# Attention and squared-ReLU FFN on one core: three score bursts instead of four in one group, and the second batch's values loaded behind w_in

## The chip, the cores and the metric

The kernel runs on one core of a Trainium2 chip. The metric is the device time of one execution in microseconds (us), as the median of several runs. The engines are named as in the profile: PE is TensorE (matmuls), PEld its weight loads, ACT is ScalarE, DVE is VectorE, POOL is GpSimd, SP is SyncE. "L367" is a line of the kernel. Lines after 570 differ by three between the two kernels; those quoted most (L341 score matmuls, L351 exponentials, L367 attention times values, "AV", L425 and L462 the first FFN matmul, L524 the second) are the same in both.

## The reference

Grouped-query attention, heads put side by side, then an FFN with a squared ReLU. Outputs and inputs are float32. (Shortened here.)

```python
def _attn_ref(q, k, v):               # q (8,16,384,64), k and v (8,4,384,64)
    k = np.repeat(k, 4, axis=1); v = np.repeat(v, 4, axis=1)
    scores = np.matmul(q, k.transpose(0, 1, 3, 2)) / np.sqrt(64)
    attn = np.exp(scores - scores.max(-1, keepdims=True))
    attn = attn / (attn.sum(-1, keepdims=True) + 1e-09)
    return np.matmul(attn, v)

def reference(q, k, v, moe_w_in, moe_w_out):      # w_in (1024,2048), w_out (2048,1024)
    a = _attn_ref(q, k, v)
    x = a.transpose(0, 2, 1, 3).reshape(8 * 384, 1024)
    h = np.maximum(x @ moe_w_in, 0.0)
    return h * h @ moe_w_out
```

## The kernel before

The program is built by a small scheduler. It appends instructions to the five engines with its own estimates of when each is ready, always takes the most urgent candidate that is ready, and picks a PSUM bank for each tile. What comes out is a fixed instruction list for each engine. So a change in one place of the source can move the order of everything after it.

A score "burst" is the set of score matmuls that one exponential reads. The first batch's attention runs at the start, with pieces of its first FFN matmul (four "early" output tiles) as filler. Then the second batch's scores are mixed with the rest of that matmul, twelve tiles in three groups of four ("quads"). Then come the second batch's AV and the first batch's second FFN matmul, and so on.

```python
    def burst_small(b, pieces, base):          # scores of some key units, then one exponential
        def sc(pe):
            for m, (u, _, _) in enumerate(pieces):
                for x in range(2):
                    mm = pe.matmul(ps[:, base + x, m * wide:(m + 1) * wide],
                                   kT[b % 2][64 * x:64 * x + 64, u, :], q_cols(b, u // NJ, x, c0, c0 + wide))
            return mm
        # ... tensor op, then on ScalarE:
        R.add("scalar", lambda e: e.activation(dst, src, AF.Exp, scale=0.125), reads=keys, ...)

    def pick(allowed):                          # which PSUM bank
        turn_count[0] += 1
        i = min(allowed, key=lambda i: (max(R.when(writes=[("bank", i)]), R.clock["tensor"]), used[i]))
        used[i] = turn_count[0]
        return i

    # ... the order of GpSimd's loads at the start
    load_q(1, 0, 8)
    load_q(1, 8, 16)
    load_w_in(1)
    load_v(1)
    dup_k(1)
    for i in range(2, 6):
        load_w_in(i)
    aug_v(1, "gpsimd")                          # waits for load_v(1)
    for i in range(6, 8):
        load_w_in(i)
    load_w_out(0, 0)
    load_w_out(0, 1)

    # ... the first batch's bursts: (key unit, first column, columns)
    for group in ((0, 1), (2, 3), (4, 5), (6, 7), (8, 9), (10, 11)):
        if 0 < group[0] < NU - 2:
            smalls += [[(u, 0, 512)] for u in group] + [[(u, 512, 256) for u in group]]
        else:
            smalls += [[(u, c0, 384)] for c0 in (0, 384) for u in group]

    # ... when an AV is taken
            b, c = av_q.pop(0)
            av_open = (b, c, av(b, c, spare))   # spare: banks that pick may choose from
```

The softmax here doesn't subtract the row's maximum and nothing guards it: scores larger than these inputs give would overflow.

## Time and profile before

| | us |
|---|---|
| median of 3 runs, known when the prediction was made | 419.39 (419.33 to 420.10) |
| median of 6 runs, with those taken beside the changed kernel | 419.75 (419.16 to 420.46) |
| the profiled execution given for it | 1111.98 |
| a later profiled execution of the same kernel, at normal speed (b_look below) | 419.48 |

For the comparisons further down I use profiles of the same kernel taken later at normal speed. The head of the page of b_look (span, then busy time, share and instructions of each engine):

```profile
span 417.4 us, 9624 instructions
PE 413.7 (99%) x4330; PEld 237.5 (57%) x4330; DVE 199.3 (48%) x434; ACT 158.9 (38%) x181; POOL 47.9 (11%) x63
```

### The profile page before, as it was taken

Reading aid. Unit: us, or ns where it says so; the run is one execution under the profiler, and the core shown is the slowest. Engines: PE = TensorE matmul, PEld = TensorE weight load, DVE = VectorE, ACT = ScalarE, POOL = GpSimd, SP = SyncE. Lnnn points to the kernel's source line nnn. Section 1 sums busy time; section 2 is a strip of 40 time slices with the busy share of each in tenths; the row PEclk is TensorE's granted clock in tenths of the full one; section 3 lists DMA queues with packets and bytes.
Section 4 is the critical chain, followed back from the end, with each engine's and each line's share of the span. In section 5 each row is a group of like instructions: output and inputs, shape, how many; then the busy total and the mean of one; then the engine's idle time right before and its main releaser. Section 6 shows DMA issues by size and latency. Waiting matters only on the chain.

```text
span 1110.1 us, 9624 instructions
## 1 busy us (share of the span) xinstructions
PE 1107.0 (100%) x4330; PEld 446.8 (40%) x4330; DVE 203.8 (18%) x434; ACT 169.6 (15%) x181; POOL 48.0 (4%) x63
## 2 busy tenths in 40 slices
PE   9999999999999999999999999999999999999999
PEld 5544523454233532345323363243632336234323
DVE  3312201131011310114001141012300123001100
ACT  5233000330023100230003300032000320001100
POOL 7100101000100010000100000000000000000000
DMA  9950626102600070000700013000110001000000
GB/s 186 203 72 1 99 53 90 15 1 49 106 16 1 9 125 29 10 1 15 119 28 10 1 22 69 29 10 0 24 34 29 1 1 29 29 28 1 0 28 29
DMA packets 96921, 44.40 MB, mean 40 GB/s; under 512 B 77296, under 2 KB 90864, under 8 KB 96880
## 3 DMA queue, kind: packets, MB, share of 16 engines
q0 software_dynamic: 36544, 17.44, 12.2%
q1 hardware_dynamic: 59664, 25.86, 9.6%
q8 instruction: 34, 0.56, 0.2%
q10 hardware_dynamic: 672, 0.49, 0.1%
q14 instruction: 7, 0.06, 0.0%
HBM read 35.65 MB, written 12.58 MB: 43 GB/s over the span
## 4 chain that ended last, share of the span: by engine, by line
PE 100%; DVE 0%; issue 0%
PE ps L524 41%; PE ps L462 35%; PE ps L367 8%; PE ps L341 8%; PE ps L425 6%; PE ps L588 1%; PE ps L315 0%; PE ps L298 0%; PE ps L400 0%; DVE y_sb L533 0%
## 5 line engine op out<-in xcount | busy, mean ns | idle before, releaser
L524 PE MATMUL ps<-w_out_sb,h2T 128*128 128x512 bf16 (+2 forms) x784 | 460.1, 823 | 0.0
L462 PE MATMUL ps<-xT,w_in_sb 64*128 64x384 bf16 x1728 | 415.1, 681 | 0.0
L524 PEld LDWEIGHTS ps<-w_out_sb,h2T 128*128 128x128 bf16 x784 | 135.6, 175 | 309.0 <-issue 308.8
L462 PEld LDWEIGHTS ps<-xT,w_in_sb 64*128 64x128 bf16 x1728 | 153.7, 170 | 232.1 <-issue 221.8
L351 ACT ACTIVATE expT<-ps 128x1024 bf16<-128x1024 f32 (+1 forms) x146 | 146.8, 1012 | 583.7 <-PE ps L341 583.6
L475 DVE TENSOR_SCALAR hr<-ps 128x384 f32<-128x384 f32 x108 | 55.2, 553 | 371.5 <-PE ps L462 371.5
L341 PE MATMUL ps<-qT,kT 64*128 64x256 bf16 (+2 forms) x384 | 114.0, 651 | 0.0
L533 DVE COPY y_sb<-ps 128x512 f32<-128x512 f32 (+2 forms) x49 | 33.4, 681 | 406.5 <-PE ps L524 406.5
L367 PEld LDWEIGHTS ps<-v_aug,expT 128*128 128x128 bf16 x1152 | 87.1, 141 | 16.5 <-issue 12.9
L367 PE MATMUL ps<-v_aug,expT 128*128 128x65 bf16 x1152 | 90.8, 281 | 0.0
L425 PE MATMUL ps<-xT,w_in_sb 128*128 128x384 bf16 x160 | 73.1, 684 | 0.0
L341 PEld LDWEIGHTS ps<-qT,kT 64*128 64x128 bf16 x384 | 29.6, 150 | 54.5 <-issue 33.7
L482 DVE TENSOR_TENSOR h2T<-hr 128x384 bf16<-128x384 f32 x102 | 50.0, 551 | 0.0
L425 PEld LDWEIGHTS ps<-xT,w_in_sb 128*128 128x128 bf16 x160 | 27.4, 173 | 41.1 <-issue 41.0
L382 DVE TENSOR_TENSOR o_sb<-ps,rinv 128x384 bf16<-128x384 f32 x64 | 35.7, 557 | 2.2
L435 ACT ACTIVATE h2T<-hr 128x384 bf16<-128x384 f32 x20 | 10.5, 523 | 137.2 <-DVE hr L433 137.2
L479 ACT ACTIVATE h2T<-hr 128x384 bf16<-128x384 f32 x6 | 3.1, 523 | 158.9 <-DVE hr L475 158.9
L275 POOL COPY v_aug<-v_st 128x768 bf16<-128x768 bf16 x8 | 6.6, 830 | 460.0 <-PE ps L367 415.2
L376 DVE RECIPROCAL rinv<-ps 128x6 f32<-128x6 f32 x64 | 12.4, 194 | 51.1 <-PE ps L367 51.1
L433 DVE TENSOR_SCALAR hr<-ps 128x384 f32<-128x384 f32 x20 | 11.2, 558 | 54.5 <-PE ps L425 54.5
L241 POOL DMA_DIRECT2D q_st<-in_q_dram x17 | 14.8, 881 | 0.9 <-POOLq L829 0.8
L209 POOL DMA_DIRECT2D k_st<-in_k_dram x7 | 5.3, 755 | 156.2 <-DMA qT<-q_st 156.2
(29 smaller groups left out, 79.3 us busy)
## 6 DMA issues: line engine op xcount, KB each, us to landing
out_dram<-y_sb SPq DMA_DIRECT2D x47, 256.0 KB, 2.0
q_st<-in_q_dram POOLq DMA_DIRECT2D x14, 384.0 KB, 7.5
w_in_sb<-in_moe_w_in_dram POOLq DMA_DIRECT2D x8, 512.0 KB, 14.3
w_out_sb<-in_moe_w_out_dram POOLq DMA_DIRECT2D x4, 1024.0 KB, 27.6
v_st<-in_v_dram POOLq DMA_DIRECT2D x8, 192.0 KB, 8.4
k_st<-in_k_dram POOLq DMA_DIRECT2D x7, 192.0 KB, 3.8
q_st<-in_q_dram POOLq DMA_DIRECT2D x3, 192.0 KB, 5.4
xT<-o_sb SPq DMA_TRANSPOSE x28, 2.7
```

The lines of the kernel that those rows point to most:

```text
L241: i = R.add("gpsimd", lambda g: g.dma_start(q_st[st][:, h0:h1, :], q[b, h0:h1].rearrange("h (p j) d -> p h (j d)", j=NJ)), writes=[("q_st" ...
L341: mm = pe.matmul(ps[:, base + x, m * wide:(m + 1) * wide], kT[b % 2][64 * x:64 * x + 64, u, :], q_cols(b, u // NJ, x, c0, c0 + wide))
L351: R.add("scalar", lambda e: e.activation(dst, src, AF.Exp, scale=0.125), reads=keys, writes=[("expT", (b * NU + u) % NEX, t) for u, _, _ i ...
L367: m = pe.matmul(po[:, f - 6 * s2, 0:D + 1], w, v_aug[b % 2][:, g * NJ + j, 0:D + 1], start=(j == 0), stop=(j == NJ - 1))
L376: R.add("vector", lambda e: e.reciprocal(rinv[r].ap().unsqueeze(2), po[:, :, D:D + 1]), reads=[("bank", i)], writes=[("rinv", r)], cost=0.22)
L382: R.add("vector", lambda e: e.tensor_tensor(dst, srcv, rbv, ALU.mult), reads=[("bank", i), ("rinv", r)], writes=[("o_sb", o, s2)], cost=0.48)
L425: m = pe.matmul(bank(i)[:, 0:S], w_in_sb[:, kc, c * 128:(c + 1) * 128], xT[b % NXT][:, kc, :], start=(kc == 0), stop=(kc == NKC - 1))
L462: m = pe.matmul(bank(4 + xs[x])[:, 0:S], w_in_sb[r, kc, c * 128:(c + 1) * 128], xT[b % NXT][r, kc, :], start=(phase < 2 and kc == 0), stop ...
L475: R.add("vector", lambda e, r=r, i=i: e.tensor_scalar_max(hr[r][:, :], bank(4 + i)[:, 0:S], 0.0), reads=[("bank", 4 + i)], writes=[("hr", ...
L482: hr_read[r] = (R.add("vector", lambda e, c=c, r=r: e.tensor_tensor(h2T[:, c, :], hr[r][:, :], hr[r][:, :], ALU.mult), reads=[("hr", r)], ...
L524: m = pe.matmul(bank(i)[:, 0:n], h2T[:, c, i3 * 128:(i3 + 1) * 128], w_out_sb[:, c, c0:c1], start=(c == 0), stop=(c == NFC - 1))
L533: R.add("vector", lambda e: e.tensor_copy(ysl, bank(i)[:, 0:n]), reads=[("bank", i)], writes=[("y", yb)], cost=0.08 + n / 960)
```

## The change

The intent: the last group of the first batch's scores takes three exponentials in place of four, so that ScalarE ends sooner; w_in's chunks come sooner, because the second batch's values, which are needed only much later, are loaded behind them; and GpSimd does not stand still before it issues w_in's last two chunks. The loads of the third batch may be issued once the first batch's transposes are done. (Some unchanged lines are left out below.)

```diff
@@ -569,13 +569,10 @@
     load_q(1, 0, 8)
     load_q(1, 8, 16)
     load_w_in(1)
+    dup_k(1)
+    for i in range(2, 8):
+        load_w_in(i)
     load_v(1)
-    dup_k(1)
-    for i in range(2, 6):
-        load_w_in(i)
-    aug_v(1, "gpsimd")
-    for i in range(6, 8):
-        load_w_in(i)
     load_w_out(0, 0)
     load_w_out(0, 1)
@@ -610,7 +607,7 @@
-        if 0 < group[0] < NU - 2:
+        if group[0] > 0:
@@ -627,7 +624,7 @@
-    chores = [([("q_st", 1, 2, 0)], lambda: turn_q_dma(1, 1))]
+    chores = [([("q_st", 1, 2, 0)], lambda: turn_q_dma(1, 1)), ([("v_st", 1)], lambda: aug_v(1, "gpsimd"))]
@@ -675,7 +672,7 @@
-        if loaded + 1 < B and turned >= loaded and not turn_q:
+        if loaded + 1 < B and turned >= loaded and not [x for x in turn_q if x[0] == 0 or loaded > 1]:
```

## The prediction

The factor of 2.76, by which the prediction divides TensorE's stretches, is 596 ns over the time of a matmul of 512 columns at normal speed; there was no trace at normal speed yet, and the author assumed that time, as 401 us of work then fit into 419. That fewer exponentials cost less is seen in its own two figures: 256 columns more take 0.20 us (0.90 less 0.70), so an exponential has some 0.10 us besides its columns (0.70 less 3 x 0.20), an estimate. The 0.98 us by which w_in is to land earlier is an estimate from 192 KB and 195 GB/s.

> **What bounds the kernel now.** I read the head of the page first, because its span does not agree with the time.
>
> ```profile
> span 1110.1 us, 9624 instructions
> PE 1107.0 (100%) x4330; PEld 446.8 (40%) x4330; DVE 203.8 (18%) x434; ACT 169.6 (15%) x181; POOL 48.0 (4%) x63
> ```
>
> The kernel is timed at 419.39 us, but the profiled execution took 1110.1. It fell in a state in which TensorE ran slow, although its granted clock is listed as 1.0. So the page's "PE 100%" is a statement about that state. Before using any wait from this trace I must separate what shrinks in a normal run (TensorE) from what does not (ScalarE, GpSimd, DMA). The chain in order of time gives the TensorE rate:
>
> ```profile
> 122.08 54.81 PE ps L524 x92
> 1050.64 57.17 PE ps L524 x112
> ```
>
> 92 matmuls of 512 columns in 54.81 us are 596 ns each. [...] The whole 1107.0 us of TensorE becomes 401 us. Of 419.39 us that leaves about 18 us in which TensorE waits or is slower than scaled: the start, the first batch, the end. Only there can this change act.
>
> The timelines of ScalarE and TensorE over the first 60 us show the first batch (starts, durations, instruction, idle time before it):
>
> ```profile
> 7.16 1.51 ACT L351 ACTIVATE expT<-ps 128x768 bf16<-128x768 f32 x2 [2.19 <-PE ps L341]
> 11.79 1.94 ACT L351 ACTIVATE expT<-ps 128x1024 bf16<-128x1024 f32 x2 [0.24 <-PE ps L341]
> ...
> 35.12 0.81 ACT L351 ACTIVATE expT<-ps 128x768 bf16<-128x768 f32 x1 [0.28 <-PE ps L341]
> 36.64 0.81 ACT L351 ACTIVATE expT<-ps 128x768 bf16<-128x768 f32 x1 [0.71 <-PE ps L341]
> ```
>
> In the trace ScalarE waits for TensorE before nearly every exponential. With TensorE 2.76 times faster this turns round: the 31 us of TensorE work between 6 and 37 us become 11.2 us, while ScalarE still needs its 20 exponentials. Where two run back to back, a 768-wide one takes 0.70 us from start to start (1.51 - 0.81) and a 1024-wide one 0.90 (another pair of 1.92 us, less 1.02). Eight of the first and twelve of the second are 16.4 us. So in a normal run ScalarE bounds the first batch's scores, from about 7.2 to 23.6 us, and TensorE idles there. What is left for TensorE after its last score burst ends with this:
>
> ```profile
> 36.10 0.50 PE L341 MATMUL ps<-qT,kT 64*128 64x384 bf16 x2
> 36.53 1.07 PE L425 MATMUL ps<-xT,w_in_sb 128*128 128x384 bf16 x2
> ...
> 46.37 8.63 PE L425 MATMUL ps<-xT,w_in_sb 128*128 128x384 bf16 x19
> 54.93 1.31 PE L341 MATMUL ps<-qT,kT 64*128 64x512 bf16 x4
> ```
>
> From 36.53 to 54.93 it is 18.4 us, scaled 6.7. I call T0 the moment at which the second batch's scores begin (54.93 here). From the ScalarE side: the last score burst can issue when its banks come free, two exponentials before the end, 23.6 - 1.4 = 22.2; plus 6.7 gives T0 = 28.9. From the other end: after T0 TensorE has 1052.9 us, scaled 381.2; 419.4 less 381.2, less 1.9 (the profiled run's 1111.98 against its span) and 2.3 for the last store, gives 34 at most. So T0 lies between 29 and 34, I work with 31; after it the kernel is TensorE's to the end. T0 earlier by x is the time shorter by x, unless a load stops it.
>
> The loads are the third thing. Their times are not scaled:
>
> ```profile
> 15.01 3.51 POOL L252 DMA_DIRECT2D w_in_sb<-in_moe_w_in_dram  x4
> 21.71 0.83 POOL L275 COPY v_aug<-v_st 128x768 bf16<-128x768 bf16 x1 [3.18 <-DMA v_st<-in_v_dram]
> 22.47 1.75 POOL L252 DMA_DIRECT2D w_in_sb<-in_moe_w_in_dram  x2
> 24.21 1.77 POOL L258 DMA_DIRECT2D w_out_sb<-in_moe_w_out_dram  x2
> ...
> DMA to landing us min/median/max: 6.8/14.3/17.5
> DMA to landing us min/median/max: 21.1/27.6/34.1
> ```
>
> The two last lines are those of w_in's 8 and w_out's 4 loads. The queue moves some 195 GB/s (of what it writes) without a pause from 2 to 64 us, so a chunk of w_in (512 KB) takes 2.7 us and 192 KB takes 0.98. The first half of w_out lands at 24.2 + 21.1 = 45.3; counting back from it, w_in's chunks 2 to 7 land at about 26.7, 29.4, 32.0, 34.7, 37.3 and 40.0 (an estimate; the median delay of 14.3 fits it).
>
> [...] k_st, v_st, w_in and w_out land in issue order as far as I can see them. [...]
>
> **The change, part by part.** (1) The last group of the first batch: four 768-wide exponentials become three 1024-wide. ScalarE: 4 x 0.70 - 3 x 0.90 = 0.10 us less. TensorE: eight matmuls of 384 columns become four of 512 and four of 256, in pairs, the same 1536 column times. The order matters more. The last burst now issues when only two exponentials of 0.90 remain instead of two of 0.70, on an end that is 0.10 earlier: 0.5 us earlier. Two of the four early output tiles may take their banks only once that last burst is out (16 of the 28 matmuls of L425 left then, 16 x 0.1625 = 2.6 us scaled). They start 0.5 us earlier, in time in which TensorE idles. Against it: the next-to-last AV needs both 512-wide pieces, so it is ready 0.9 before ScalarE's end, not 1.4: 0.4 later. The last AV is ready 0.1 earlier. As TensorE has filler for both gaps, T0 should come 0.1 to 0.5 earlier; I take 0.35.
>
> (2) The load of the second batch's values goes behind w_in: chunks 2 to 7 land 0.98 us earlier, w_out as before. With T0 = 31 the first quad of tiles needs chunk 2 at 31 and chunk 3 a quarter quad later (32.3), and they land at 26.7 and 29.4 already; a quad is 5.2 us and with its score bursts about 6.3, so chunks 4 and 6 are needed at 37 and 44 and land at 32.0 and 37.3. Nothing waits, so the gain is near 0 unless T0 is below 28. I add 0.15 for that.
>
> (3) GpSimd loses the wait of 3.18 us in front of w_in's chunks 6 and 7. They are issued earlier, but the DMA queue was never empty, so it is worth 0. The copy into v_aug now comes after the values land, at about 41, and is first used by the second batch's AV, after three quads (T0 + 19 = 50). Hidden.
>
> (4) The looser condition for the third batch's loads puts them ahead of that copy in GpSimd's order, so the copy does not hold them up. In the trace they are issued from 25.94 on, right behind w_out; nothing gets later. Worth 0.
>
> Sum: 0.35 + 0.15 = 0.5 us, 418.9.
>
> **The rivals.** First, w_out catches it: its last part lands at 27.6 + 34.1 = 61.7 and is needed about T0 + 33 = 64. Transposes and stores that in a normal run come while the queue is still busy could delay it to that point; then any gain at T0 is lost again there, and the time stays at 419.4. For it: only 2 us of slack by estimate. Against it: in the trace no matmul waits for w_out at all, but it ran late. Second, w_in binds: if T0 is really near 28, chunk 3 is on the path and both parts count, up to 1.4 us, 418.0. For it: the author moved the load. Against it: the count of 34 from the other end. Third, the later next-to-last AV costs more than the earlier filler saves, since its division, transposes and copy precede work on the path: plus 0.4, 419.8. Fourth, the order is made by a scheduler with its own estimates; another order at the switch can cost or save a few tenths anywhere.
>
> **Range and chances.** The first and third rival set the top, the second the bottom: 418.0 to 419.8. Two per cent is 8.4 us; no part handles more than the 18 us at the edges, and none moves over 1.4. I give 0.98 to the same.
>
> **What would show it.** In the changed kernel: 15 exponentials of 1024 and 4 of 768 in the first batch; no GpSimd wait before w_in's chunks 6 and 7; v_aug's second copy near 41 us; landings of w_in about 1 us earlier, of w_out unchanged. In a profile at normal speed: ScalarE near full between 8 and 24 us, no TensorE wait for w_in before the first quad, T0 near 31. A wait of TensorE for w_in or w_out of over 0.5 us would prove part 2 or the first rival wrong; a time below 418 would mean that w_in was on the path.

## The result, and the profile after

The changed kernel took 419.88 us (median of 6 runs, 419.35 to 420.55), beside 419.75 for the kernel before (6 runs). The ratio is 1.0003, with a 95% interval of 0.9987 to 1.0018: no difference. (A ratio is the mean time of one kernel's fast runs over that of the other's fast runs in the same rounds, so it is not quite the ratio of the medians.) The predicted gain of 0.5 us did not come, and 419.88 lies 0.08 us above the predicted range. Of the 0.99 us between 418.89 and 419.88, 0.36 is the base, whose median of three runs was 419.39 and of six 419.75; 0.5 is the gain that did not come; 0.13 is the difference of the medians.

The head of its page:

```profile
span 418.7 us, 9600 instructions
PE 412.9 (99%) x4307; PEld 235.9 (56%) x4330; DVE 199.3 (48%) x434; ACT 158.9 (38%) x180; POOL 48.0 (11%) x63
```

ScalarE has 180 instructions in place of 181: the one exponential less. The chain in order of time gives the normal rate of TensorE, in answer to the two lines that the prediction showed (the second of those holds shorter matmuls too, so its mean is not that of 512 columns). From start to start the 512-column matmuls of L524 are 216 ns apart here (50 in 10.79 us):

```profile
57.04 10.74 PE ps L524 x49
374.78 20.80 PE ps L425 x128
```

128 matmuls of 384 columns in 20.80 us are 162.5 ns each; in the slow profile 128 of them took 57.16 us, 446.6 each. So the factor for long matmuls was 2.75; the prediction took 2.76. (A few matmul records are missing: 4307 of 4330. Hence 49 where 50 ran.)

GpSimd's timeline shows part 2 of the change:

```profile
15.62 5.26 POOL L252 DMA_DIRECT2D w_in_sb<-in_moe_w_in_dram  x6
21.56 1.83 POOL L258 DMA_DIRECT2D w_out_sb<-in_moe_w_out_dram  x2
42.50 0.83 POOL L275 COPY v_aug<-v_st 128x768 bf16<-128x768 bf16 x1 [14.09 <-DMA v_st<-in_v_dram]
```

The six chunks of w_in are issued in one go, the wait in the midst of them is gone, and the copy into v_aug comes at 42.5, where 41 was forecast. The first half of w_out lands 26.0 us after its issue, at 47.6.

The step that I doubted most was ScalarE and TensorE at the end of the first batch. ScalarE's timeline of the changed kernel:

```profile
5.83 1.51 ACT L351 ACTIVATE expT<-ps 128x768 bf16<-128x768 f32 x2 [0.72 <-PE ps L341]
8.10 15.27 ACT L351 ACTIVATE expT<-ps 128x768 bf16<-128x768 f32 x17 [0.75 <-PE ps L341]
```

and TensorE's, from the last score burst of the first batch to the second batch's first (T0):

```profile
21.73 0.39 PE L341 MATMUL ps<-qT,kT 64*128 64x256 bf16 x4
22.06 0.34 PE L400 MATMUL ps<-ident,o_sb 128*128 128x128 bf16 x3
22.24 0.33 PE L425 MATMUL ps<-xT,w_in_sb 128*128 128x384 bf16 x1
22.50 0.72 PE L367 MATMUL ps<-v_aug,expT 128*128 128x65 bf16 x18
23.06 0.33 PE L400 MATMUL ps<-ident,o_sb 128*128 128x128 bf16 x3
23.23 0.33 PE L425 MATMUL ps<-xT,w_in_sb 128*128 128x384 bf16 x1
23.42 0.72 PE L367 MATMUL ps<-v_aug,expT 128*128 128x65 bf16 x18
...
26.03 3.41 PE L425 MATMUL ps<-xT,w_in_sb 128*128 128x384 bf16 x20
29.38 0.60 PE L341 MATMUL ps<-qT,kT 64*128 64x512 bf16 x4
```

ScalarE runs without a break from 8.10 to 23.37. (The gap before 8.10 is the start: the second load of keys landed at 6.66 us in this execution, at 5.13 to 5.32 in the later ones of the changed kernel proper.) Between the last burst at 21.73 and ScalarE's end TensorE has no room: one AV, two groups of three transposes and two early matmuls follow each other closely. Here is the same stretch of the kernel before, from b_look, in which ScalarE's 20 exponentials ran from 5.62 to 22.35:

```profile
21.12 0.34 PE L341 MATMUL ps<-qT,kT 64*128 64x384 bf16 x2
21.39 0.50 PE L425 MATMUL ps<-xT,w_in_sb 128*128 128x384 bf16 x2
21.72 0.71 PE L367 MATMUL ps<-v_aug,expT 128*128 128x65 bf16 x18
22.27 0.33 PE L400 MATMUL ps<-ident,o_sb 128*128 128x128 bf16 x3
22.44 0.71 PE L367 MATMUL ps<-v_aug,expT 128*128 128x65 bf16 x18
...
25.15 3.25 PE L425 MATMUL ps<-xT,w_in_sb 128*128 128x384 bf16 x19
28.33 0.61 PE L341 MATMUL ps<-qT,kT 64*128 64x512 bf16 x4
```

In both kernels the last AV starts just after ScalarE's end (23.42 after 23.37, 22.44 after 22.35), and in both 26 of the 32 early matmuls (L425) come after it. So the distance from ScalarE's end to T0 is fixed: 5.97 us with four bursts and 6.01 with three, in every profile at normal speed.

After T0 the order of TensorE's instructions is the same in both kernels to the end. A difference after T0 can thus only be a wait. The changed kernel has one that no rival of the prediction named (the first two lines; the third is the same place in b_look, where the AVs run through):

```profile
53.15 1.01 PE L367 MATMUL ps<-v_aug,expT 128*128 128x65 bf16 x28
54.43 0.40 PE L367 MATMUL ps<-v_aug,expT 128*128 128x65 bf16 x8 [0.26 <-issue]
```

```profile
52.27 1.26 PE L367 MATMUL ps<-v_aug,expT 128*128 128x65 bf16 x36
```

In the middle of an AV TensorE stands still, and "issue" says that it waits for nothing that the profile shows.

### The profile page after: what moved, and what is told of

It reads as the page before. It is cut to its first block, busy times and chain, and to the rows that moved or that the text cites. A ratio compares the mean times of both kernels' runs of the same rounds, so it can differ in the third digit from the quotient of the medians.

```text
span 418.7 us, 9600 instructions
## 1 busy us (share of the span) xinstructions
PE 412.9 (99%) x4307; PEld 235.9 (56%) x4330; DVE 199.3 (48%) x434; ACT 158.9 (38%) x180; POOL 48.0 (11%) x63
## 4 chain that ended last, share of the span: by engine, by line
PE 97%; DMA 1%; issue 0%; ACT 0%; DVE 0%; POOL 0%; ACTq 0%
PE ps L524 39%; PE ps L462 34%; PE ps L367 9%; PE ps L341 8%; PE ps L425 6%; DMA k_f<-in_k_dram 1%; PE ps L400 0%; PE ps L315 0%; ACT expT L351 0%; PE ps L298 0%; DVE qT L322 0%; POOL k_dup L270 0%; ACTq L223 0%; DVE y_sb L533 0%; PE ps L585 0%
## 5 line engine op out<-in xcount | busy, mean ns | idle before, releaser
L524 PE MATMUL ps<-w_out_sb,h2T 128*128 128x512 bf16 (+2 forms) x761 | 165.7, 374 | 1.2
L462 PE MATMUL ps<-xT,w_in_sb 64*128 64x384 bf16 x1728 | 160.0, 323 | 0.0
L524 PEld LDWEIGHTS ps<-w_out_sb,h2T 128*128 128x128 bf16 x784 | 75.1, 98 | 86.6
L462 PEld LDWEIGHTS ps<-xT,w_in_sb 64*128 64x128 bf16 x1728 | 83.3, 94 | 57.3 <-DVE hr L475 2.1
L341 PE MATMUL ps<-qT,kT 64*128 64x256 bf16 (+2 forms) x384 | 54.1, 326 | 0.1
L367 PEld LDWEIGHTS ps<-v_aug,expT 128*128 128x128 bf16 x1152 | 36.9, 98 | 5.9 <-DVE hr L475 1.6
L367 PE MATMUL ps<-v_aug,expT 128*128 128x65 bf16 x1152 | 39.0, 193 | 0.3 <-issue 0.3
L425 PE MATMUL ps<-xT,w_in_sb 128*128 128x384 bf16 x160 | 27.5, 326 | 0.0
L341 PEld LDWEIGHTS ps<-qT,kT 64*128 64x128 bf16 x384 | 17.7, 94 | 15.1 <-issue 2.4
L425 PEld LDWEIGHTS ps<-xT,w_in_sb 128*128 128x128 bf16 x160 | 15.5, 98 | 9.8
```

The lines of the kernel that those rows point to most:

```text
L341: mm = pe.matmul(ps[:, base + x, m * wide:(m + 1) * wide], kT[b % 2][64 * x:64 * x + 64, u, :], q_cols(b, u // NJ, x, c0, c0 + wide))
L367: m = pe.matmul(po[:, f - 6 * s2, 0:D + 1], w, v_aug[b % 2][:, g * NJ + j, 0:D + 1], start=(j == 0), stop=(j == NJ - 1))
L425: m = pe.matmul(bank(i)[:, 0:S], w_in_sb[:, kc, c * 128:(c + 1) * 128], xT[b % NXT][:, kc, :], start=(kc == 0), stop=(kc == NKC - 1))
L462: m = pe.matmul(bank(4 + xs[x])[:, 0:S], w_in_sb[r, kc, c * 128:(c + 1) * 128], xT[b % NXT][r, kc, :], start=(phase < 2 and kc == 0), stop ...
L524: m = pe.matmul(bank(i)[:, 0:n], h2T[:, c, i3 * 128:(i3 + 1) * 128], w_out_sb[:, c, c0:c1], start=(c == 0), stop=(c == NFC - 1))
```

## The experiments

Every kernel below gave a correct result. All but five were timed in five rounds beside the kernel before on the same chip; those five had one look (one run with a profile, whose state cannot be told; the granted clock was 1.0 in four of them and 0.996 in a_act_plus3). I count four things in each profile, from its records: T0 less the start of the first exponential; TensorE's wait for w_in in the first quad; the stall in L367; and the stretch from T0 to the start of the last copy of the output, which holds everything after T0.

Among the DMA packets are some of kind instruction: one queue (q8) carries 34 packets of 16,384 bytes in each execution, another (q14) a few small ones. TensorE's list has 8711 instructions (two for each of 4330 matmuls, and 51 others). I take the 34 packets for TensorE's and call them so below. That is an estimate from these counts: 8711/34 would be 256 instructions to a packet. What a packet holds, and what starts it, is not in the trace.

**First set: both kernels again, and each part alone.** The three bursts alone (p1) and the values behind w_in alone (p2):

```diff
 p1, against the kernel before          p2, against the changed kernel
-        if 0 < group[0] < NU - 2:      -        if group[0] > 0:
+        if group[0] > 0:               +        if 0 < group[0] < NU - 2:
```

The fourth line of the change, the looser condition for loads, needed no run: built with the old condition, the changed kernel has the same instructions in the same order on all five engines (only numbers of semaphores differ, and the order in which one copy names its two waits). So it does nothing here.

> The kernel before, again, for its profile at normal speed and as a null comparison. Theory (the switch bounds nothing new): ratio 1.000, spread of single times about 1.2 us as in the record; exponentials of the first batch back to back from about 8 us; the second batch's scores begin (T0) 0.1 us after those of the changed kernel's profile (29.4) when the keys land at the same time; 26 of the 32 matmuls of L425 left after ScalarE's last exponential, as in the changed kernel. Rival (the change gains at T0 and loses it later): T0 0.3 to 0.5 us later than in the changed kernel, and the stretch from T0 to the end shorter by as much.

> The changed kernel, again. Theory: ratio 0.999 to 1.001; T0 minus the start of the third exponential 21.3 us as in its first profile (29.4 less 8.1); the single times differ with the landing of the second keys' load (6.7 us in its first profile, 5.2 in the slow one of before), which moves the third exponential. Rival (loss after T0): T0 to the end longer than in the kernel before by 0.3 us or more.

> The three bursts alone, values loaded where they were. The scheduler then orders eleven of the second batch's score bursts a half or whole quad part later. Theory (ScalarE's end sets T0, and it ends 0.1 us earlier): T0 minus the third exponential 0.1 less than in the kernel before, time equal within 0.2 us. Rival (w_in is on the path once T0 is earlier): TensorE waits for w_in at the first or second quad, 0.3 to 1 us longer than the changed kernel.

> Only the values behind w_in and the copy as a chore, four bursts kept. TensorE's and ScalarE's order is that of the kernel before. Theory: w_in chunks 2 to 7 land 1.0 us earlier than in the kernel before, no matmul waits for them in either, time equal within 0.2 us. Rival (w_in binds): 0.3 to 1 us faster than the kernel before.

Measured: b_again 420.16 us, ratio 1.0017 (1.0005 to 1.0029); a_again 419.69, 1.0005 (0.9993 to 1.0017); p1 419.70, 1.0009 (0.9996 to 1.0022); p2 419.75, 1.0002 (0.9990 to 1.0014); the kernel before in these rounds 419.38. The first is the same program as its comparison, and its interval does not hold 1. So five rounds do not tell apart what differs by 0.2%, and the traces must decide.

b_again shows a wait for w_in in the first quad:

```profile
29.05 1.46 PE L462 MATMUL ps<-xT,w_in_sb 64*128 64x384 bf16 x16
30.93 0.83 PE L462 MATMUL ps<-xT,w_in_sb 64*128 64x384 bf16 x8 [0.41 <-DMA w_in_sb<-in_moe_w_in_dram]
```

Its chunk 3 landed at 30.79 and was needed at T0 + 1.74 = 30.35; the pair started 0.58 us later than without a wait. In p2, where the chunk landed at 28.84, there is no such wait, nor any stall. p1 did not wait either, against the rival's expectation: its chunk landed at 29.97, 0.3 us before its need. (p1's T0 came 23.10 us after the first exponential, later than in the kernel before and not 0.1 sooner as expected.) a_again has the stall again, longer:

```profile
53.51 0.40 PE L367 MATMUL ps<-v_aug,expT 128*128 128x65 bf16 x8 [0.66 <-issue]
```

The records of weight loads, laid beside those of p2 from T0 on, put the loss at this one place: 0.43 us in the first profile of the changed kernel, 0.83 in a_again, 0.42 in p1, always at TensorE's instruction 1474. There b_again loses 0.09. In all that have three bursts TensorE's instruction packet begins 3.15 to 3.4 us after the first AV, in the two with four bursts 2.65 to 2.75.

**Second set: is it ScalarE's count, and how close is w_in?** A second small instruction packet also came 0.85 us later with three bursts (T0 + 20.2 against T0 + 19.35). My guess was that ScalarE's count of instructions, lower by one, brings both this and the stall. Two kernels give the changed one idle copies on ScalarE, one takes an instruction from ScalarE in the kernel before, and one puts 192 KB more ahead of w_in:

```diff
 a_act_plus3, in the changed kernel (a_act_plus1: the same with one copy; the tile's definition is left out)
+    for n in range(3):
+        R.add('scalar', lambda e, n=n: e.copy(idle_act[:, n:n + 1], k_f32[:, 0, 0:1]), reads=[('k_f32', 0)], cost=0.0)
 b_act_minus1, in the kernel before
-    R.add("vector", lambda e: e.tensor_copy(q_to[:, 0:192], q_from[:, 0:192]), ...)
-    for n in range(2):
+    R.add("vector", lambda e: e.tensor_copy(q_to[:, 0:384], q_from[:, 0:384]), ...)
+    for n in range(1, 2):
 b_values_twice, in the kernel before
     load_w_in(1)
+    R.add("gpsimd", lambda g: g.dma_start(v_twice..., v[1]...), dma="v_twice", cost=0.0, issue=0.0)
     load_v(1)
```

> The changed kernel with one idle one-element copy on ScalarE in front of its first exponential, so that ScalarE has as many instructions as in the kernel before. TensorE's order is unchanged. Seen so far, from T0 (start of the second batch's scores): the second small packet of kind instruction at T0 + 20.2 us in the three kernels with three bursts, at T0 + 19.35 (w_in wait taken off) in the two with four; TensorE's own 16 KB instruction packet at T0 + 22.8 to 23.0 against 22.3; and only in those with three bursts TensorE stalls 0.25 to 0.66 us in L367 with nothing to wait for. Theory[...]: the packets return to T0 + 19.35 and 22.3, the stall goes, T0 to the last copy 386.6 to 386.8 us instead of 387.0 and 387.4. Rival (the stall comes from TensorE's own changed order before T0, or from traffic): it stays, 0.25 to 0.7 us.

> The same with three idle copies. Theory: the small packet two score bursts (2 x 0.87 us) earlier again, at about T0 + 17.6; no stall in L367; T0 itself up to 0.3 us later if the copies are in the way of the first exponential. Rival: packet where it was, stall as in the changed kernel.

> The kernel before with one ScalarE instruction less (the first 192 columns that ScalarE casts go into VectorE's cast). TensorE's order is that of the kernel before. Theory: small packet at T0 + 20.2 (any w_in wait taken off), TensorE's packet at about T0 + 22.9, and now a stall of 0.25 to 0.7 us in L367, which the kernel before does not have. Rival (TensorE's order makes the stall): none. Second question: w_in's chunk 3 waited for by 0.3 to 0.8 us if T0 is under 29, as in the profile of the kernel before.

> The kernel before with the second batch's values loaded twice (once to a tile nobody reads), 192 KB or 0.98 us more ahead of w_in's chunks 2 to 7. Theory (chunk 3 is at the edge in the kernel before): TensorE waits 1.3 to 1.9 us for w_in in the first quad, the first AV of the second batch comes 21 to 21.5 us after T0 instead of 20.19 and, without any wait, 19.61. Prediction on record (1.5 us of slack): no wait over 0.3.

Measured: a_act_plus1 420.06 us, ratio 1.0011 (0.9989 to 1.0033). The small packet did return to T0 + 19.3, but TensorE's packet stayed at 3.20 us after the first AV, and the stall at 0.44 us. In a_act_plus3 the small packet moved to T0 + 16.9 and the stall was 0.73. In b_act_minus1 the small packet moved to T0 + 20.2, and there was no stall. So the guess about ScalarE fell: its count moves the small packet, and the stall does not follow it. The rival stands: something in TensorE's own list. (a_act_plus3 took 423.0 us. TensorE waited 1.6 us for a load of queries there, and T0 came 25.57 us after the first exponential, against 22.7 undisturbed (1.3 us and 23.94 in a_act_plus1); a single look of unknown state, and I conclude nothing from its time.)

b_values_twice (419.65 for the kernel before, 420.08 for it):

```profile
28.73 1.46 PE L462 MATMUL ps<-xT,w_in_sb 64*128 64x384 bf16 x16
30.94 0.83 PE L462 MATMUL ps<-xT,w_in_sb 64*128 64x384 bf16 x8 [0.75 <-DMA w_in_sb<-in_moe_w_in_dram]
```

The chunk landed at 30.81, and the quad lost 0.92 us. That is less than the 1.3 to 1.9 that I had written down, as b_again, from which I had started, was itself a late one, but far from the slack that the prediction had.

**Third set: the banks.** What differs in TensorE's list after T0, when the order is the same? The waits. With one burst less, the scheduler's count of turns gives other banks to the second batch's AVs: 5, 1, 4, 2, 3, 0, 5, 1 in place of 0, 3, 5, 4, 1, 2, 0, 3. Bank 5 has just held a quad's tile, so the first AV waits for VectorE to read it; bank 0 has held scores, so it waits for an exponential. The weight load of the first AV says so (the changed kernel, then b_look):

```profile
48.98 1.09 PEld L367 LDWEIGHTS ps<-v_aug,expT 128*128 128x128 bf16 x34 [0.32 <-DVE hr L475]
```

```profile
48.11 1.97 PEld L367 LDWEIGHTS ps<-v_aug,expT 128*128 128x128 bf16 x63 [0.32 <-ACT expT L351]
```

Neither delays the AV itself: in both it starts 19.61 us after T0, unless w_in was waited for. But VectorE's read ends 0.39 us before the AV and the exponential 0.94 before, 0.55 apart; over all profiles the instruction packet is 0.5 later on average (3.24 against 2.74). To test it I set the banks by hand, in both directions, all eight at once; no engine's order changes:

```diff
-            av_open = (b, c, av(b, c, spare))
+            av_open = (b, c, av(b, c, (((0, 3, 5, 4, 1, 2, 0, 3)[c]),) if b == 1 else spare))   # in the changed kernel
+            av_open = (b, c, av(b, c, (((5, 1, 4, 2, 3, 0, 5, 1)[c]),) if b == 1 else spare))   # in the kernel before
```

> The changed kernel with the eight PSUM banks of the second batch's AVs set to those of the kernel before (0, 3, 5, 4, 1, 2, 0, 3 for 5, 1, 4, 2, 3, 0, 5, 1); every engine's order stays. The theory that ScalarE's count of instructions does it has fallen. Theory now: in the changed kernel the first AV's bank 5 makes TensorE's sequencer wait for VectorE's read of the quad before (done at T0 + 19.2), in the kernel before bank 0 makes it wait for an exponential (done 0.5 us earlier)[...]. So here: wait of the first AV's weight load put down to ScalarE, instruction packet at T0 + 22.2 to 22.4 instead of 22.8 to 23.0, no stall in L367 over 0.1, T0 to the last copy 386.5 to 386.7. Rival (traffic, or something else in the three bursts): packet at 22.8, stall 0.4 to 0.8 stays. In the time: 0.4 us less than the changed kernel, below what five rounds resolve.

> The reverse: the kernel before with the banks of the changed one. Theory: wait of the first AV put down to VectorE, instruction packet 22.8 to 23.0 us after T0 (any w_in wait taken off), stall of 0.4 to 0.8 us at instruction 1474. Rival: none, as in the kernel before.

> The kernel before once more, for how often it waits for w_in: its chunk 3 is needed 1.74 us after T0. If it lands before that (about 30.1 for T0 = 28.4), no wait and T0 to the last copy 386.6; if after, a wait of the difference. Theory: within 0.6 us of the edge either way. Prediction on record (slack of 1.5 to 3 us): never a wait.

> Four bursts, values behind w_in, again: neither wait. T0 to the last copy 386.5 to 386.7 as before; chunk 3 lands 1.0 us or more ahead of its need. Time not told from the kernel before by five rounds: ratio 0.998 to 1.001.

Measured: the changed kernel with the banks of before took 419.27 us, ratio 0.9993 (0.9980 to 1.0006). Its packet began 2.80 us after the first AV, and the AV runs through (first AV's weight load; then the place of the stall, now 36 matmuls in one piece):

```profile
48.54 1.54 PEld L367 LDWEIGHTS ps<-v_aug,expT 128*128 128x128 bf16 x49 [0.32 <-ACT expT L351]
```

```profile
52.70 1.30 PE L367 MATMUL ps<-v_aug,expT 128*128 128x65 bf16 x36
```

The kernel before with the banks of the changed one (one look, 419.53 us) has the packet at 3.22 us and the stall, 0.47 us in the comparison of records:

```profile
47.76 2.33 PEld L367 LDWEIGHTS ps<-v_aug,expT 128*128 128x128 bf16 x75 [0.32 <-DVE hr L475]
```

```profile
53.25 0.40 PE L367 MATMUL ps<-v_aug,expT 128*128 128x65 bf16 x8 [0.31 <-issue]
```

b_look waited 0.18 us for w_in (chunk 3 landed at 30.11, needed at 30.07). p2_again had neither wait, and took 419.59 us, ratio 0.9999 (0.9985 to 1.0013).

**Fourth set: the times.** The changed kernel, the changed kernel with the banks of before, and the kernel before, on one chip in the same rounds:

> The changed kernel on one chip beside the version with the banks of before. Theory: instruction packet 3.15 to 3.4 us after the second batch's first AV, stall of 0.4 to 0.9 us in L367, none for w_in, T0 to the last copy 387.0 to 387.4. In time 0.4 us over the next kernel's, about 0.001 of ratio, so perhaps within the intervals.

> The changed kernel with the banks of before, on the same chip. Theory: packet 2.65 to 2.85 us after the first AV, no stall over 0.1, T0 to the last copy 386.6; median time 0.4 us under the changed kernel's and 0.1 to 0.4 under that of the kernel before. Rival (one of the two stalls was chance): no difference in the trace.

> The kernel before as its own control on the same chip. Theory: wait for w_in of 0 to 0.6 us, no instruction stall over 0.1, ratio 1.000 but by experience up to 0.002 off for the same program.

Measured, with the kernel before at 419.84 in these rounds: a_third 419.65 us, ratio 0.9998 (0.9985 to 1.0012); a_banks_again 419.16, ratio 0.9987 (0.9973 to 1.0000); b_third, the kernel before once more, 419.44, ratio 0.9990 (0.9976 to 1.0004). The means of the six runs of a_third and a_banks_again are 419.74 and 419.25, 0.49 apart (95% interval from these twelve times, my working: 0.08 to 0.90); their traces say 0.46 (387.04 less 386.58). One expectation failed: b_third lost 0.36 us at instruction 1474, though it has the banks of before. Its packet began 2.92 us after the AV, later than in the other profiles of that bank order. So with those banks the stall is mostly, but not always, absent (0 to 0.09 us in the other eight profiles). Its ratio of 0.9990 for an unchanged program also shows how little 0.9987 says.

The account, all in us ("ahead": values loaded ahead of w_in; "5...": banks 5, 1, 4, ... for the second batch's AVs):

| profile | bursts | values | banks | T0 - first exp | wait for w_in | packet after AV | stall | T0 to last copy |
|---|---|---|---|---|---|---|---|---|
| b_again | 4 | ahead | 0... | 22.84 | 0.58 | 2.65 | 0.09 | 387.25 |
| b_look | 4 | ahead | 0... | 22.71 | 0.18 | 2.72 | 0 | 386.76 |
| b_third | 4 | ahead | 0... | 22.73 | 0.18 | 2.92 | 0.36 | 387.12 |
| b_act_minus1 | 4 | ahead | 0... | 22.70 | 0 | 2.75 | 0 | 386.59 |
| b_values_twice | 4 | ahead, twice | 0... | 22.74 | 0.92 | 2.64 | 0.02 | 387.52 |
| b_banks_as_after | 4 | ahead | 5... | 22.73 | 0.02 | 3.22 | 0.47 | 387.07 |
| p1 | 3 | ahead | 5... | 23.10 | 0 | 3.15 | 0.42 | 387.00 |
| p2, p2_again | 4 | behind | 0... | 22.70, 22.70 | 0, 0 | 2.75, 2.80 | 0, 0 | 386.58, 386.62 |
| changed | 3 | behind | 5... | 23.55 | 0 | 3.25 | 0.43 | 387.00 |
| a_again | 3 | behind | 5... | 22.70 | 0 | 3.37 | 0.83 | 387.41 |
| a_third | 3 | behind | 5... | 22.74 | 0 | 3.23 | 0.47 | 387.04 |
| a_act_plus1 | 3 | behind | 5... | 23.94 | 0 | 3.20 | 0.44 | 387.02 |
| a_act_plus3 | 3 | behind | 5... | 25.57 | 0 | 3.26 | 0.73 | 387.31 |
| a_banks_as_before | 3 | behind | 0... | 23.34 | 0 | 2.80 | 0 | 386.61 |
| a_banks_again | 3 | behind | 0... | 22.83 | 0 | 2.65 | 0 | 386.58 |

In every row the last column is 386.6 plus the wait for w_in plus the stall. (p1's order of score bursts differs after T0, the others' does not.) The stall's own size can be taken apart too. From the first AV, undisturbed, the instruction that stalls comes 5.01 us later (b_look). In the nine profiles with a stall it issues 2.19 to 2.49 us after the packet's start, so a stall is the packet's delay after the AV, plus this time, less 5.01. The two longest, 0.83 and 0.73, and those of b_third and b_again have 2.45 to 2.49; the other five have 2.19 to 2.29. In the profiles of the 0... banks without a stall it is 2.26 to 2.38. Whether the instruction that stalls came with this packet is not shown.

## Why the prediction was wrong

The class, no change by 2%, was right, and so was the broad frame: TensorE binds after T0, and only waits count. The gain of 0.5 us did not come: its first term was 0, its second stood on a wrong step, and a cost was missing.

**"In time in which TensorE idles"** failed. It rested on dividing TensorE's 31 us by 2.76. That factor holds for long matmuls (2.75 measured) but not for short ones: one AV, 18 matmuls of 65 columns, took 1.32 us from start to start in the slow profile and 0.65 at normal speed, a factor of 2.0; a score burst, from its start to that of the next instruction, went from 0.62 to 0.32. From the first score burst to the last, 29.5 us of the slow profile (6.62 to 36.10) became 15.9 (5.25 to 21.12), where the division gives 10.7 us of work. ScalarE paces that stretch too, so its length alone proves little; but in b_look TensorE is busy for 15.37 of its 15.87 us, and its weight loads wait for ScalarE's exponentials for 1.4 us in all. With hardly any idle time, bursts that issue some 0.4 us sooner before ScalarE's end bring no filler forward: in both kernels 26 early matmuls are left there.

**"ScalarE: ... 0.10 us less"** was right in kind and too large: the undisturbed stretches of exponentials are 16.73 to 16.77 us with four bursts and 16.69 and 16.73 with three, and the distance to T0 grew by 0.04. From the first exponential to T0 it is 22.70 us with either. The term of 0.35 is 0.

**"I work with 31" and "nothing waits"** failed. The lower bound of T0 in the prediction, 28.9, was nearly right: undisturbed it is 28.1 to 28.6. I then took a value from the middle of the bracket, though the upper bound counted everything that was unexplained as time before T0 (it had 381.2 us after T0, where the traces show 386.6 to the last copy). Two smaller errors went the same way: chunk 3 lands at 29.8 to 30.8 in the kernel before instead of 29.4, and is needed 1.74 us after T0 instead of 1.3. So a slack of 2.9 us was in truth 0.3 to -0.4, and the second rival ("if T0 is really near 28, chunk 3 is on the path") had the mechanism. Part 2 of the change does remove a wait: 0.58, 0.18 and 0.18 us in the three profiles of the kernel before (0, 0 and 0.02 in b_act_minus1, p1 and b_banks_as_after, which load in the same order), none in any with the values behind. The 0.15 set down for it comes near by luck: it was an allowance for a case held to be unlikely. With 192 KB more ahead of w_in, in b_values_twice, the wait was 0.92 us, the longest.

**What was missing from the list of rivals** is where this gain went: a new wait. The three bursts shift the scheduler's choice of banks, the first AV then waits for VectorE's read instead of an exponential, and TensorE stands still before its instruction 1474 for 0.42 to 0.83 us. That the banks make the difference is shown, by setting them in both directions: 0.42 to 0.83 in seven profiles with the one order, 0 to 0.36 in nine with the other. (The fourth rival came nearest: the scheduler did cost a few tenths, but through banks and not through another order.) How they do so is not shown: the release is 0.55 us later and the packet begins 0.5 later, but nothing in the trace tells what starts the packet. As the eight banks were set together, it is not shown either that the first AV's wait alone does it, though up to the packet only the first AV's weight loads show a wait. The stall varies with the packet's start (3.15 to 3.37 us after the AV) and with the time from there to the stalled instruction (2.19 to 2.49); why the latter varies stays open.

Together: the wait removed is 0 to 0.6 us and the stall added 0.4 to 0.8, so the two about cancel: from T0 to the last copy the three profiles of the kernel before average 387.04 us and those of the changed one 387.15. Ratios of 1.0003, 1.0005 and 0.9998 fit that, but could not show it. The other rivals fell: the second part of w_out is waited for in no profile, and the next-to-last AV costs nothing, as T0 follows ScalarE's end by the same 6 us.

**The range** was also too narrow for the base. Executions of one program reach T0 up to 1.3 us apart: the second load of keys landed at 6.66 us in the changed kernel's profile and at 5.13 in a_again's, and T0 was 29.38 and 28.06. A base known from three runs within 0.8 us did not show that.

The changed kernel with the banks of before has neither wait: 419.27 and 419.16 us. Against the changed kernel on one chip it is 0.49 us faster, as its trace says; against the kernel before its ratios are 0.9993 and 0.9987, and neither interval lies clearly below 1. Its trace after T0 is no shorter than that of p2 (386.61 and 386.58 us against 386.58 and 386.62), which keeps all of the change but the three bursts and sets no banks by hand. So by the traces the moved loads are worth keeping, and the three bursts brought nothing and cost the stall.

## What to carry to other kernels

When a large part of a profile runs at a different speed, scale each kind of instruction by its own factor, and where a bracket comes out, test the conclusion at both of its ends instead of at the middle. In a program laid out by a scheduler, compare the wait lists and the buffers after a change, not only the order: an edit of one burst moved a bank choice 27 us later. A bank that costs nothing where it is first used may still go with a stall further on: the first AV began 19.61 us after T0 with either set of banks, and with one of them TensorE stood still for 0.42 to 0.83 us some 5 us later (that the banks make it is shown here, how is not). Where a stall is put down to "issue", the starts of the instruction packets are worth comparing; here they were 0.5 us apart on average (3.24 and 2.74 us after the first AV).
